# A sigmoid attention with a SwiGLU block: who issues the loads of v, one transfer for each load, and the order inside the first quad

## The chip, the cores and the metric

The kernel runs on one NeuronCore of a Trainium2 chip. The metric is the device time of one execution in microseconds; lower is better. In this document PE is TensorE (PEld its weight loads), DVE is VectorE, ACT is ScalarE, SP is SyncE. SP does no arithmetic here: it issues almost all DMAs, one after the other, in the order in which the program lists them.

## The reference

```python
scores = (q @ k.T) / sqrt(64) - log(448)          # for each of 4 batches and 12 heads, 448 positions
attn   = sigmoid(scores)                          # no softmax, so no sum over a row
x      = (attn @ v), heads side by side           # 1792 tokens x 768
xn     = x / sqrt(mean(x*x) + 1e-6) * rms_g
out    = (silu(xn @ w_gate) * (xn @ w_val)) @ w_out   # d_ff 1536
```

q, k and v come as float32, the weights as 64-bit words that the kernel turns into float32 itself.

## The kernel before, in words

**Units.** Four heads of one batch make a unit; there are 12, u = 0 to 11. Two heads lie side by side on the partitions (r = 0, 1 are the two pairs of heads of a unit). For each unit the kernel loads q and k (`load_qk`, lines 192 to 193) and v (`load_v`, lines 200 to 201). Both go through `load` (lines 186 to 190), which makes two DMAs, one for each r, of 224 KB each, both on SP. Unit 0 alone takes its q and k by `load_first` (lines 195 to 198), in pieces that hold both r at once, 128 to 256 KB.

**q and k on their way.** DVE splits them into two float16 parts (`qk_hi` L227, `qk_lo` L231). The parts are then transposed: for the first units on PE (`on_pe`, L263), from unit 3 on by one DMA transpose for each unit (`transpose_both`, L234), issued by SP too. I call these transposes T(3) to T(11). `scores` (L282) needs the transposed tile.

**Steps.** Each unit has 7 steps (c = 0 to 6). The main loop (lines 900 to 922) takes two steps at a time: first the scores of steps n and n+1 (24 small PE products), each followed on ACT by a sigmoid (L286), then the products with v of steps n-2 and n-1 (`av`, L297, 16 products). The scores have two PSUM buffers ("sc"), so the scores of step s wait for the sigmoid of step s-2. Between steps stand the parts of the list `FILL` (lines 853 to 861: the splits, transposes and loads of later units) and whatever `run_later` (lines 805 to 820) draws by its credits from the queues of additions, norms and weight splits.

**v.** There are two buffers for v, `v_b[u % 2]`. When the last product of unit u is listed, `av` calls `load_v(u + 2)` (lines 307 to 308). The load waits until that product has been done. On SP it is listed behind what was listed earlier: T(u+2) at step 3 of unit u, then k and q of unit u+4 at step 4, and only then v of unit u+2. Right behind the call the squares and scaled copies of the unit that just ended are run on ACT (`evict`, L316 and L319).

**Quads.** After the attention, 24 quads (one for each block of 128 columns of d_ff and each of two groups of batches) compute gate and value by seven products in place of eight (`quad`, lines 543 to 617; one product is nine PE instructions, L532). A quad takes its first product into the PSUM tile `pb` ("cb"), runs `fill(0)`, takes the second into the same tile, runs `fill(1)`, takes the third into `pd` ("cd"), runs `fill(2)`, takes the fourth into `pa` ("ca"), and so on. In the first quad, (0, 0), `fill` (lines 933 to 944) runs the norm of the last batch: `fill(0)` begins with its sums of squares on PE (`ssq`, L354), which need additions on DVE (L322) that follow the last products of the attention, and `fill(2)` holds the PE product that spreads the norm (`rinv`, L392).

**Start.** Lines 878 to 893 list the first loads on SP: q and k of unit 0 in pieces, v of unit 0, q and k of unit 1, the norm's weights, then units 2, 3 and the first weights.

Of the kernel before, what the change touches and what calls it, by code (L numbers as in the profile page):

```python
# [24 lines left out]
def attention_then_swiglu(  # L25
# [21 lines left out]
    nc = tc.nc  # L47
    B, H, S, D = q.shape
    DFF, DM = w_out.shape
    P = 128  # L50
# [53 lines left out]
    def words(of, at, *shape, dt=F32):  # L104
        n = math.prod(shape) if dt != F16 else math.prod(shape) // 2
        t = of[:, at : at + n]
        if dt != F32:
            t = t.bitcast(dt)
        names = " ".join("abcdef"[: len(shape)])
        sizes = dict(zip("abcdef", shape))  # L110
        return t.rearrange(f"p ({names}) -> p {names}", **sizes)
# [19 lines left out]
    v_b = [words(room, at0 + n * UW // 2, 2, NSLOT, D) for n in range(2)]  # L131
# [41 lines left out]
    def bank(name):  # L173
        return ps_m.tile([P, 512], F32, tag="m", name=name)

    def banks(name):
        return ps_s.tile([P, 2, 512], F32, tag="sc", name=name)
# [5 lines left out]
    at, pav = {}, {}  # L183
    PARTS = ((0, 0), (0, 1), (1, 0))

    def load(src, dst, u):
        b, n = divmod(u, NPAIR // 2)
        for r in range(2):
            rows = src[b, 4 * n + 2 * r : 4 * n + 2 * r + 2].rearrange("h s d -> (h s) d")
            nc.sync.dma_start(dst[:, r], rows.rearrange("(p c) d -> p c d", p=P))  # L190

    def load_qk(u, t):
        load((q, k)[t], (raw_b if u < 2 else ld_b)[u % 2][:, t], u)

    def load_first(t, *pieces):
        rows = (q, k)[t][0, :4].rearrange("(r h) s d -> r (h s) d", r=2).rearrange("r (p c) d -> p r c d", p=P)
        for begin, n in pieces:
            nc.sync.dma_start(raw(0, t)[:, :, begin : begin + n], rows[:, :, begin : begin + n])

    def load_v(u):  # L200
        load(v, v_b[u % 2], u)


    g_row = x_b[2][:NCC, 0, :P]
# [15 lines left out]
    def raw(u, t):  # L220
        return (raw_b if u < 2 else ld_b)[u % 2][:, t]
# [68 lines left out]
    def av(u, c):  # L290
        a = at.pop((u, c))
        if c == 0:
            pav[u] = [bank("av") for _ in range(2)]
        for r, ps in enumerate(pav[u]):
            for j in range(2):
                rows = slice(PB * j, PB * j + PB)
                nc.tensor.matmul(  # L297
                    ps[D * (j ^ r) : D * (j ^ r) + D, :S],
                    v_b[u % 2][rows, r, c],
                    a[rows, r],  # L300
                    start=(c == 0),
                    stop=(c == NSLOT - 1),
                )
        if c == NSLOT - 1:
            for r, ps in enumerate(pav.pop(u)):
                evict(u, r, ps)
            if u + 2 < NU:
                load_v(u + 2)
# [214 lines left out]
    def run_behind():  # L523
        if behind:
            behind.pop(0)()

    def product(ps, fc, n, a, b, more=False):

        w = win[fc % 2]
        for c in range(NK):  # L530
            for m, (l, r) in enumerate(PARTS):
                nc.tensor.matmul(  # L532
                    ps,
                    w[:, l, b, c],
                    xc[n, a][:, r, c],
                    start=(not more and c == 0 and m == 0),
                    stop=(c == NK - 1 and m == 2),
                    skip_group_check=more,
                )

    y_of = []

    def quad(fc, n, fill, whole=False):
        y = y_b[len(y_of) % 3]
        y_of.append((fc, n))
        pb = bank("cb")
        product(pb[:, :S], fc, n, 0, 0)
        nc.scalar.activation(y[:, 0], pb[:, :S], AF.Copy)  # L548
        run_behind()
        run_behind()  # L550
        fill(0)
        run_behind()

        product(pb[:, :S], fc, n, 4, 5, True)
        nc.scalar.activation(y[:, 1], pb[:, :S], AF.Copy)  # L555
        run_behind()
        fill(1)
        pd = banks("cd")[:, 0]
        product(pd[:, :S], fc, n, 5, 2)
        run_behind()  # L560
        fill(2)

        pa = bank("ca")

        def m2():
            product(pa[:, :S], fc, n, 1, 1)

        def gate():
            tt(g_b, pa[:, :S], y[:, 0], ALU.add)

        def silu():
            nc.scalar.activation(g_b, g_b, AF.Silu, scale=UNIT)

        def m7():
            product(pb[:, :S], fc, n, 3, 4, True)
            nc.scalar.activation(c_b, pb[:, :S], AF.Copy)  # L576

        def c22():
            tt(c_b, pd[:, :S], c_b, ALU.add)

        def m4():
            product(pb[:, :S], fc, n, 6, 3, True)
            stt(y[:, 0], pb[:, :S], SH * UNIT, g_b, ALU.mult, ALU.mult)

        def m3():
            product(pd[:, :S], fc, n, 2, 6, True)
            tt(y[:, 1], pd[:, :S], y[:, 1], ALU.add)  # L587

        def silu_1():
            nc.scalar.activation(y[:, 1], y[:, 1], AF.Silu, scale=UNIT)  # L590

        def ends():
            stt(y[:, 1], c_b, SH * UNIT, y[:, 1], ALU.mult, ALU.mult)
            i, m = fc % 2, fc // 2
            nc.sync.dma_start(
                y_d[n * NTOK : n * NTOK + NTOK, :, i, m].rearrange("t p x -> p t x"),
                y.rearrange("p j s -> p (j s)").rearrange("p (t x) -> p t x", x=P),
            )

        if whole:  # L600
            m7()
            c22()
            m2()
            gate()
            silu()
            fill(3)
            m4()
            m3()
            fill(4)
            behind.extend((wait, wait, wait, silu_1, ends))  # L610
        else:
            m2()
            fill(3)
            m7()
            gate()
            fill(4)
            behind.extend((silu, c22, m4, lambda: (m3(), silu_1()), ends))
# [215 lines left out]
    K, Q = 1, 0  # L833
# [36 lines left out]
    with tc.manual_schedule():  # L870
# [7 lines left out]
        warm(WARM)  # L878
        load_first(Q, *PIECES)
        load_first(K, *K_PIECES)  # L880
        load_v(0)
        load_qk(1, Q)
        load_qk(1, K)
        load_g()
        load_qk(2, K)
        load_qk(2, Q)
        load_v(1)
        load_w(0, 0)
        load_w(0, 1)
# [10 lines left out]
        for n in range(0, len(todo) + 2, 2):  # L900
# [14 lines left out]
            if n in SPLIT_AT:  # L915
                fc = SPLIT_AT.index(n)
                split[fc] = split_w(fc)
                first, second = split[fc]
                splits.extend(first[:4])
            if n in REST_AT:  # L920
                first, second = split[REST_AT.index(n)]
# [11 lines left out]
        def fill_norm(where):  # L933
            left = LEFT[where]

            def fill(at):
                run_load()
                while len(later) > left[at]:
                    later.pop(0)[0]()
                for part, *_ in third[: EARLIER[where][at]]:  # L940
                    part()
                del third[: EARLIER[where][at]]

            return fill
# [3 lines left out]
        def fill_steps(*steps):  # L948
            def fill(at):
                for p in steps[at]:  # L950
                    if p == fed[0]:
                        load_a(p, 0)
                        fed[0] += 1
                    else:
                        for part in split_a(p, 0):
                            part()

            return fill

        def fill_with(*steps):  # L960
            def fill(at):
                run_load()
                run_load()
                for part, *_ in steps[at]:
                    part()

            return fill
# [4 lines left out]
        for fc, n in order:  # L972
            if (fc, n) in LEFT:
                fill = fill_norm((fc, n))
            elif (fc, n) == (1, 1):
                assert len(third) == 8
                fill = fill_with(third[:2], third[2:4], third[4:7], third[7:], [])
            elif fc + 1 < NFC:
                first, second = split[fc + 1] = split_w(fc + 1) if n == 0 else split[fc + 1]
# [13 lines left out]
                fill = fill_with(*parts)  # L993
            elif n == 0:
                assert not outs
                fill = fill_steps([0, 1, 2], [], [0, 3, 1], [2], [4, 5])
            else:
                fill = fill_steps([3, 6], [], [4], [], [5, 6])
# [78 lines left out]
```

## Time and profile before

| | |
|---|---|
| time, median of 3 runs | 572.67 us (570.92 to 573.28) |
| the profiled execution's own time | 572.34 us |
| its span, first to last instruction | 570.5 us |
| outside the span | 1.84 us |
| PE busy | 561.1 us, 98% |
| DVE busy | 437.8 us, 77% |
| ACT busy | 265.6 us, 47% |
| PE clock granted | 1.00 throughout |
| attention | 5 to 135 us |
| quads | 135 to 423 us |
| output product | 423 to 570 us |

The attention is the stretch in which all engines and the DMAs work beside each other; in the quads and the output product PE runs without a break. A line of a timeline gives the start, the duration, the engine and line, and in brackets how long the engine had been idle before it and who ended that. For a DMA the duration on SP is the time of issuing, not of the transfer.

### The profile page before, as it was taken

Reading aid. Unit: us, or ns where it says so; the run is one execution under the profiler, and the core shown is the slowest. Engines: PE = TensorE matmul, PEld = TensorE weight load, DVE = VectorE, ACT = ScalarE, POOL = GpSimd, SP = SyncE. Lnnn points to the kernel's source line nnn. Section 1 sums busy time; section 2 is a strip of 40 time slices with the busy share of each in tenths; the row PEclk is TensorE's granted clock in tenths of the full one; section 3 lists DMA queues with packets and bytes.
Section 4 is the critical chain, followed back from the end, with each engine's and each line's share of the span. In section 5 each row is a group of like instructions: output and inputs, shape, how many; then the busy total and the mean of one; then the engine's idle time right before and its main releaser. Section 6 shows DMA issues by size and latency. Waiting matters only on the chain.

```text
span 570.5 us, 10232 instructions
## 1 busy us (share of the span) xinstructions
PE 561.1 (98%) x4224; PEld 305.2 (54%) x4224; DVE 437.8 (77%) x577; ACT 265.6 (47%) x398; POOL 0.7 (0%) x6
## 2 busy tenths in 40 slices
PE   8999989999999999999999999999999999999997
PEld 5555545554555555555555555555556666666664
DVE  4898889989886777878778787787567987777751
ACT  5788888885544243252442524425438342222220
POOL 0000000000000000000000000000000000000000
PEclk9999999999999999999999999999999999999999
DMA  7999999990017446364563745633426476444211
GB/s 247 258 260 230 224 258 236 197 207 1 19 48 198 139 148 172 103 186 131 154 169 102 192 126 157 168 99 94 143 73 220 141 227 200 150 151 143 59 41 43
DMA packets 99201, 87.25 MB, mean 153 GB/s; under 512 B 38735, under 2 KB 92242, under 8 KB 99154
## 3 DMA queue, kind: packets, MB, share of 16 engines
q1 hardware_dynamic: 98594, 85.91, 57.3%
q8 instruction: 33, 0.54, 0.4%
q10 hardware_dynamic: 560, 0.69, 0.3%
q14 instruction: 14, 0.11, 0.1%
HBM read 61.34 MB, written 16.52 MB: 136 GB/s over the span
## 4 chain that ended last, share of the span: by engine, by line
PE 90%; DVE 4%; DMA 3%; ACT 1%; SPq 1%; issue 1%; ACTq 0%; DVEq 0%
PE cb L532 28%; PE cd L532 14%; PE av L297 8%; PE oc L735 7%; PE o L735 7%; PE od L735 7%; PE ca L532 7%; PE sc L282 6%; PE ob L735 4%; DVE room L396 1%; DMA room<-in_v_dram 1%; DMA room<-in_q_dram 1%; DMA xc<-in_k_dram 1%; SPq L190 1%; ACT room L286 1%; PE ssq L354 1%
## 5 line engine op out<-in xcount | busy, mean ns | idle before, releaser
L532 PEld LDWEIGHTS <-wr 128*128 128x128 f16 x1512 | 147.8, 98 | 138.6 <-issue 1.0
L532 PE MATMUL cb<-xc,wr 128*128 128x448 f16 x756 | 147.3, 352 | 0.0
L286 ACT ACTIVATE room<-sc 128x896 f32<-128x896 f32 x84 | 75.2, 929 | 18.4 <-PE sc L282 17.7
L297 PE MATMUL av<-room 64*64 64x448 f32 x672 | 74.7, 538 | 1.4 <-DMA room<-in_v_dram 1.4
L532 PE MATMUL cd<-xc,wr 128*128 128x448 f16 x324 | 65.2, 352 | 0.0
L282 PE MATMUL sc<-xc 64*64 64x448 f16 x1008 | 59.9, 351 | 1.7 <-ACT room L286 1.0
L282 PEld LDWEIGHTS <-xc 64*64 64x64 f16 x1008 | 32.5, 106 | 30.9 <-issue 19.0
L587 DVE TENSOR_TENSOR room<-cd,room 128x448 f32<-128x448 f32 x24 | 15.0, 625 | 43.1 <-PE cd L532 43.1
L735 PEld LDWEIGHTS <-xc 128*128 128x128 f16 x360 | 35.2, 98 | 23.3
L502 DVE SCALAR_TENSOR_TENSOR wr<-wr 128x1536 f16<-128x1536 f32 (+3 forms) x28 | 37.3, 1355 | 12.5 <-ACT wr L499 12.5
L532 PE MATMUL ca<-xc,wr 128*128 128x448 f16 x216 | 44.8, 352 | 0.0
L735 PE MATMUL o<-room,wr 128*128 128x384 f16 x252 | 41.1, 326 | 0.0
L297 PEld LDWEIGHTS av<-room 64*64 64x64 f32 x672 | 27.8, 133 | 24.2 <-issue 16.9
L555 ACT ACTIVATE room<-cb 128x448 f32<-128x448 f32 x24 | 13.1, 544 | 53.8 <-PE cb L532 53.8
L576 ACT ACTIVATE room<-cb 128x448 f32<-128x448 f32 x24 | 13.1, 544 | 50.6 <-PE cb L532 30.6
L735 PEld LDWEIGHTS <-room 128*128 128x128 f16 x270 | 26.4, 98 | 17.5
L590 ACT ACTIVATE room<-room 128x448 f32<-128x448 f32 x24 | 13.8, 577 | 43.2 <-DVE room L587 43.2
L499 ACT ACTIVATE wr<-wr 128x768 f16<-128x768 f32 (+1 forms) x48 | 33.5, 754 | 0.0
L735 PEld LDWEIGHTS <-wr 128*128 128x128 f16 x252 | 24.7, 98 | 16.3
L690 ACT ACTIVATE xc<-xc 128x1536 f16<-128x1536 f32 (+1 forms) x12 | 14.5, 1260 | 36.2 <-DVE xc L687 36.2
L496 DVE TENSOR_TENSOR wr<-wr 128x384 f32<-128x384 f32 x48 | 26.4, 552 | 0.7
L548 ACT ACTIVATE room<-cb 128x448 f32<-128x448 f32 x24 | 13.1, 545 | 25.5 <-PE cb L532 25.5
(98 smaller groups left out, 676.0 us busy)
## 6 DMA issues: line engine op xcount, KB each, us to landing
y_d<-room SPq DMA_DIRECT2D x24, 448.0 KB, 3.3
xc<-in_moe_w_out_dram SPq DMA_DIRECT2D x12, 768.0 KB, 6.3
xc<-y_d SPq DMA_DIRECT2D x22, 384.0 KB, 4.4
room<-in_v_dram SPq DMA_DIRECT2D x24, 224.0 KB, 4.2
out_dram<-room SPq DMA_DIRECT2D x49, 96.0 KB, 2.2
wr<-in_moe_w_gate_dram SPq DMA_DIRECT2D x12, 384.0 KB, 4.5
wr<-in_moe_w_gate_dram SPq DMA_DIRECT2D x24, 192.0 KB, 5.0
wr<-in_moe_w_val_dram SPq DMA_DIRECT2D x12, 384.0 KB, 5.7
```

What stands on the lines that cost most here:

```text
L282: nc.tensor.matmul(o, T[rows, 1, l, c, cols], T[rows, 0, m, :, cols], start=(n == 0), stop=(n == 2))
L286: nc.scalar.activation(a, ps[:, :, :S], AF.Sigmoid, bias=-math.log(S), scale=1.0 / (math.sqrt(D) * SQ * SQ))
L297: nc.tensor.matmul(ps[D * (j ^ r) : D * (j ^ r) + D, :S], v_b[u % 2][rows, r, c], a[rows, r], start=(c == 0), stop=(c == NSLOT - 1),)
L496: first.append((lambda o=o, f0=f0, f1=f1: tt(wf[:, o], wf[:, f0], wf[:, f1], ALU.subtract), 0.6))
L499: nc.scalar.activation(t[:, 0, s], wf[:, s], AF.Copy, scale=SW)
L502: stt(t[:, 1, s], wf[:, s], SW, t[:, 0, s], ALU.mult, ALU.subtract)
L532: nc.tensor.matmul(ps, w[:, l, b, c], xc[n, a][:, r, c], start=(not more and c == 0 and m == 0), stop=(c == NK - 1 and m == 2), skip_group ...
L548: nc.scalar.activation(y[:, 0], pb[:, :S], AF.Copy)
L587: tt(y[:, 1], pd[:, :S], y[:, 1], ALU.add)
L590: nc.scalar.activation(y[:, 1], y[:, 1], AF.Silu, scale=UNIT)
L690: return lambda: nc.scalar.activation(s[:, 0, a:b], f[:, a:b], AF.Copy), 0.0, ()
L735: nc.tensor.matmul(ps[:, :HALF], a(m, l), w(m, r), start=(not more and m == 0 and n == 0), stop=(m == NM - 1 and n == 2), skip_group_check ...
```

## The change

Three things are changed. `load` makes one DMA for both r, and takes the queue as an argument; v of the units 4 to 8 is issued by ACT, at the place in the program where SP issued it. At the start q of unit 1 is listed ahead of v of unit 0. In the first quad the product into `pd` is taken second, with `fill(0)` run after its first three of nine instructions, and `fill(2)` moves behind the product into `pa`.

```diff
-    def load(src, dst, u):
+    def load(src, dst, u, queue=nc.sync):
         b, n = divmod(u, NPAIR // 2)
-        for r in range(2):
-            rows = src[b, 4 * n + 2 * r : 4 * n + 2 * r + 2].rearrange("h s d -> (h s) d")
-            nc.sync.dma_start(dst[:, r], rows.rearrange("(p c) d -> p c d", p=P))
+        rows = src[b, 4 * n : 4 * n + 4].rearrange("(r h) s d -> r (h s) d", r=2)
+        queue.dma_start(dst, rows.rearrange("r (p c) d -> p r c d", p=P))
...
     def load_v(u):
-        load(v, v_b[u % 2], u)
+        load(v, v_b[u % 2], u, nc.scalar if 3 < u < 9 else nc.sync)
...
-    def product(ps, fc, n, a, b, more=False):
+    def product(ps, fc, n, a, b, more=False, mid=None):
...
                     skip_group_check=more,
                 )
+            if c == 0 and mid:
+                mid()
...
         product(pb[:, :S], fc, n, 0, 0)
         nc.scalar.activation(y[:, 0], pb[:, :S], AF.Copy)
-        run_behind()
-        run_behind()
-        fill(0)
-        run_behind()
+        pd = banks("cd")[:, 0]
+        first = not y_of[1:]
+        if first:
+            product(pd[:, :S], fc, n, 5, 2, mid=lambda: fill(0))
+        else:
+            run_behind()
+            run_behind()
+            fill(0)
+            run_behind()
 
         product(pb[:, :S], fc, n, 4, 5, True)
         nc.scalar.activation(y[:, 1], pb[:, :S], AF.Copy)
         run_behind()
         fill(1)
-        pd = banks("cd")[:, 0]
-        product(pd[:, :S], fc, n, 5, 2)
-        run_behind()
-        fill(2)
+        if not first:
+            product(pd[:, :S], fc, n, 5, 2)
+            run_behind()
+            fill(2)
...
             m2()
+            if first:
+                fill(2)
             fill(3)
             m7()
             gate()
...
         load_first(K, *K_PIECES)
+        load_qk(1, Q)
         load_v(0)
-        load_qk(1, Q)
         load_qk(1, K)
```

## Rows read from the trace of the kernel before

**Rows 1.** Windows view, 56 to 86 us: stretch, length, busy time of each engine, clock, DMA.
```profile
56.00:86.00 30.00, 27.82 (x379) 15.49 (x371) 25.85 (x36) 25.98 (x40) 0.00 (x0) 1.00 1.11 244
```

**Rows 2.** Timeline of PE, 62 to 101 us: start, us, line, idle before and releaser.
```profile
62.79 1.30 PE L282 MATMUL sc<-xc 64*64 64x448 f16 x24
...
69.90 0.76 PE L282 MATMUL sc<-xc 64*64 64x448 f16 x12 [0.61 <-ACT room L286]
...
72.31 1.33 PE L282 MATMUL sc<-xc 64*64 64x448 f16 x24
...
77.71 2.03 PE L297 MATMUL av<-room 64*64 64x448 f32 x14 [1.43 <-DMA room<-in_v_dram]
...
97.39 1.30 PE L282 MATMUL sc<-xc 64*64 64x448 f16 x24
...
100.03 1.30 PE L282 MATMUL sc<-xc 64*64 64x448 f16 x24
```

**Rows 3.** Timeline of all engines at two places, 65 and 86 us.
```profile
65.12 0.14 PEld L297 LDWEIGHTS av<-room 64*64 64x64 f32 x2 [0.30 <-DMA room<-in_v_dram]
...
86.20 1.33 PE L282 MATMUL sc<-xc 64*64 64x448 f16 x24
```

**Rows 4.** Timeline of SP's queue, 48 to 80 us: duration is the time of issuing.
```profile
48.62 7.65 SPq L234 DMA_TRANSPOSE xc<-room  x1
...
59.25 0.85 SPq L190 DMA_DIRECT2D room<-in_v_dram  x2
...
62.42 7.88 SPq L234 DMA_TRANSPOSE xc<-room  x1
70.36 1.04 SPq L190 DMA_DIRECT2D xc<-in_k_dram  x2
...
72.45 0.85 SPq L190 DMA_DIRECT2D room<-in_v_dram  x2
73.39 6.14 SPq L234 DMA_TRANSPOSE xc<-room  x1
```

**Rows 5.** Source view of L234, the transpose issued at 62.42 alone.
```profile
DMA to landing us min/median/max: 9.8/9.8/9.8
```

**Rows 6.** Timeline of ACT, 54 to 82 us.
```profile
54.08 0.54 ACT L316 ACTIVATE room<-av 128x448 f32<-128x448 f32 x1 [1.31 <-PE av L297]
...
65.25 0.55 ACT L316 ACTIVATE room<-av 128x448 f32<-128x448 f32 x1
...
66.76 0.92 ACT L286 ACTIVATE room<-sc 128x896 f32<-128x896 f32 x1 [0.44 <-PE sc L282]
...
80.79 1.73 ACT L286 ACTIVATE room<-sc 128x896 f32<-128x896 f32 x2 [1.76 <-PE sc L282]
```

**Rows 7.** Source views of L198 and L797: issue durations ns, min/median/max.
```profile
L198 SPq DMA_DIRECT2D room<-in_q_dram x2: 450/455/460, 0.7 to 1.3; - x2
...
L797 ACTq DMA_DIRECT2D out_dram<-room x7: 496/497/557, 479.3 to 567.0; - x7
```

**Rows 8.** Timeline at 552 us: one DMA issue on SP and one on ACT.
```profile
552.42 0.47 SPq L797 DMA_DIRECT2D out_dram<-room  x1
552.42 0.50 ACTq L797 DMA_DIRECT2D out_dram<-room  x1
```

**Rows 9.** Timelines of PE and DVE, 135 to 141 us, the first quad.
```profile
135.00 1.88 PE L532 MATMUL cb<-xc,wr 128*128 128x448 f16 x9
137.24 0.95 PE L354 MATMUL ssq<-ones,room 128*112 128x1 f32 x8 [0.37 <-DVE room L322]
138.05 1.86 PE L532 MATMUL cb<-xc,wr 128*128 128x448 f16 x9
139.75 1.87 PE L532 MATMUL cd<-xc,wr 128*128 128x448 f16 x9
...
136.56 0.63 DVE L322 TENSOR_TENSOR room<-room,xc 128x448 f32<-128x448 f32 x1
```

**Rows 10.** Timeline of DVE at 10 us: the first split of q of unit 1.
```profile
9.97 0.63 DVE L227 TENSOR_SCALAR room<-room 128x896 f16<-128x896 f32 x1 [0.19 <-DMA room<-in_q_dram]
```

## The prediction

> **What bounds the kernel now.** I read the busy time by stretch first. From the quads on PE has no gap, so only the attention and the seam to the first quad can give anything. In the attention the stretch from 56 to 86 us is the poor one: PE is busy for 27.82 of 30 us, and ACT for 25.98 [rows 1], so ACT is close behind PE. The timeline of PE tells what a pair of steps costs when nothing is late: 100.03 - 97.39 = 2.64 us [rows 2]. Between 62.79 and 86.20 [rows 2, 3] PE does seven pairs, 7 x 2.64 = 18.48, and eight sums of squares (about 0.8, as 138.05 - 137.24 in [rows 9]), 19.3 in all; it takes 23.41. So 4.1 us are lost there. The brackets name the losers: PE waits 0.30 for v of unit 5 at 65.12, 0.61 for ACT at 69.90, and 1.43 for v of unit 6 at 77.71 [rows 2, 3].
>
> Then SP's queue, to see why v is late. The products of unit 4 were done by 65.25, when ACT squared them [rows 6]; from then on v of unit 6 could be loaded. It was issued at 72.45, because the transpose T(6) held SP from 62.42 to 70.30 and k and q of unit 8 came next [rows 4]. So 7.2 us of lateness are the queue's order, not the transfer's.
>
> Last, ACT. From its sigmoid at 66.76, late by 0.44 since v of unit 5 had upset the order of products on PE, it works without idling until 80.79 - 1.76 = 79.03, then idles 1.76 because PE stood waiting for v [rows 6]. What PE can gain here is therefore what ACT's chain of 79.03 - 66.76 = 12.27 us allows.
>
> **v of units 4 to 8 on ACT.** v of unit 6 is issued at about 65 in place of 72.45 and lands well before 76. Unit 5's is issued at 54 in place of 59.25. With v of unit 5 in time, PE takes the next scores 2.64 after 62.79, at 65.43, and the sigmoid that began at 66.76 has its 12 products some 0.75 later, at 66.2: 0.57 earlier. ACT's 12.27 us then end at 78.5, and with no wait for v the next sigmoid starts there, not at 80.79: 2.3 gained. PE also ran its products out of step from 78 to 84; with those in step I take 2.8 of the 4.1. Bounds: 1.8 (ACT loses only its idle time of 1.76), 4.1 (all).
>
> The price on ACT is five issues of 0.50 [rows 7]. For v of unit 6 ACT must wait until PE has done unit 4, then issues, and its square at 65.25 comes hardly later. At 54.08 ACT had idled 1.31 waiting for PE, so the issue falls behind that wait and delays the square by 0.5, of which about half reaches PE through the next sigmoid. Each of the five lies between 0 and 0.5; I take 0.15 on average, 0.75 together. v of unit 4 lands in time too, which gives back 0.35, about one group of four products (a quarter of 1.5). No row shows an issue on ACT beside a transpose on SP; the third rival prices that.
>
> **One transfer for each load.** The nearest row for the issue of a transfer of both r is `load_first`'s 0.455 [rows 7]; two halves cost 0.85 to 1.04 [rows 4]. SP gets back about 0.5 for each k and q, and all of v's 0.85 where ACT issues it. Before T(6) that is k and q of unit 7 and v of unit 5, 1.9, and as much again before T(5), for k and q of unit 6 and v of unit 4: T(6) is issued some 3 us earlier. T(6) landed at 62.42 + 9.8 = 72.2 and PE's scores at 72.31 had waited for it [rows 2, 4, 5]. v of unit 6 now crosses while T(6) is under way; its 448 KB at the 244 GB/s of this stretch [rows 1] are 1.9 us of the engines. 3 - 1.9 still leaves T(6) about 1 us ahead, which is what the 2.8 needs. If the transfers bind and T(6) stays at 72.2, only 1.8 remain. The bytes and the size of their pieces don't change, so the DMA engines get nothing back. A product with v now waits for both r, which costs nothing where v is early. From 86 on PE is dense and T(8) to T(11) move with SP.
>
> **q of unit 1 ahead of v of unit 0.** DVE waited 0.19 for that q [rows 10]; it is first on the queue now. 0.2 gained; bounds 0 and 0.2. v of unit 0 lands where q did, 9.94, over 2 us before its first product.
>
> **First quad.** PE idles before `ssq`, which waits for an addition that ends at 137.19. A product takes 139.75 - 138.05 = 1.70, so the first one ended at 136.70 and 0.54 were lost [rows 9] (the row's bracket says 0.37, since it lets the last product end later). Three of the nine instructions of the moved product, 0.57, fill the gap: `ssq` starts at 137.27. Nothing is added: the same nine are gone from their old place. `rinv` comes about as late as before (1.70 + 0.57 + 0.8 + 1.13 + 1.70 + 1.70 = 7.6 after 135.00, so 142.6 against 141.45); ACT and DVE use it only behind other work. 0.5 gained; bounds 0.3 and 0.55. If DVE should lag PE by more, the cover of 0.57 is too short and the rest of the lag is paid as before.
>
> **Sum.** 2.8 + 0.35 - 0.75 + 0.2 + 0.5 = 3.1. The profiled execution took 572.34 (span 570.5 and 1.84 around it), 0.33 below the median of the runs shown. 572.34 - 3.1 = **569.2**. A measurement of this kernel can tell about 0.5% from no change, 2.9 us; against the median that is below 569.8.
>
> **Rivals.**
> 1. *The transfers bind.* T(6) comes no earlier, since v of unit 6 shares the engines with it. For it: a DMA share above 1 in this stretch [rows 1]. Against it: SP issues without a break, so the queue's order alone explains the lateness. Then 1.8 replaces 2.8: 570.2, no change.
> 2. *ACT becomes the bound.* The issues are not hidden: 5 x 0.5 = 2.5 in place of 0.75, while ACT is busy 26 of 30 us [rows 1]. Then 572.34 - 1.35 = 571.0, no change.
> 3. *ACT's issue waits for SP's transpose.* Where SP is inside a transpose, ACT would stand until that has been issued: at 54.08 until 48.62 + 7.65 = 56.27, at 65.25 until 70.30, and for v of unit 7, about 10 us later at 75.3, until 73.39 + 6.14 = 79.53 [rows 4, 6]: 2.2 + 5.0 + 4.2 = 11.4 on an engine that is the next bound. ACT's idle times cover 1.31 + 0.44 + 1.76 = 3.5 of it, and the 0.7 of the last two parts stay: 572.34 + 7.9 - 0.7 = 579.5, slower. It decides as soon as the issue on ACT takes more than about 1 us. Against it: at 552.42 SP and ACT issue at the same time, 0.47 and 0.50, neither longer than alone [rows 7, 8]; but neither is a transpose, and with T moved ahead by 3 us the waits shrink. The Trainium skill, Perfetto Trace Analysis, section "DMA Instruction — HWDGE (DVE, Sync)", says that the block which makes the descriptors is shared by two sequencers and locked by one for its own use; by that rule this rival is the forecast and the time is its 579.5, but the two equal rows at 552.42 don't show it.
> 4. *The loads are as late as before.* If ACT reached its issue no earlier than SP did, nothing in the attention would move: 572.34 - 0.7 = 571.6. Nothing speaks for it, as ACT's square at 65.25 stands right behind the place of the issue.
>
> **Chances.** Forecast 0.52 (from 567.3, with all of the 4.1, the price on ACT down to 0.2 and 0.55 in the quad, to 569.8), rival 1 0.18, rival 2 0.14, rival 3 0.12, rival 4 0.04. The range of 8 in 10 takes in rivals 1, 2 and 4, which end at 571.6, and a share of the noise: 567.3 to 572.2. Faster by over 0.5%: 0.52; within 0.5%: 0.36; slower: 0.12.
>
> **What would show it.** Right: in the new trace the five issues on ACT take about 0.5 each, v of unit 6 is issued near 65 and PE has no wait for v; the pair of steps that began at 86.20 begins near 83.6 (86.20 less 2.8 + 0.35 - 0.75 + 0.2); SP's transpose T(6) begins near 59; `ssq` follows the three products without idling. Wrong: an issue on ACT of several us (rival 3); PE waiting for the transposed tile near 72 (rival 1); PE waiting longer for ACT at 48 to 60 and near 70 (rival 2).

## The result, and the profile after

| | kernel before | changed kernel |
|---|---|---|
| time, median of 12 runs each, on the same chip | 572.5 us (569.81 to 574.81) | 575.46 us (574.16 to 578.22) |
| ratio to before, 95% interval | | 1.0051 [1.0032, 1.0071] |
| the profiled execution: time, span | 572.34, 570.5 us | 575.54, 573.8 us |

The changed kernel is slower by 0.5%. The forecast was 569.2, with a range up to 572.2: wrong in sign and outside the range.

The windows view of the changed kernel, with the columns of [rows 1], shows in which stretch the time goes.

```profile
20.00:56.00 36.00, 34.49 (x506) 18.49 (x501) 29.92 (x58) 28.59 (x42) 0.00 (x0) 1.00 1.16 246
56.00:86.00 30.00, 25.24 (x338) 12.30 (x334) 22.93 (x33) 23.21 (x37) 0.00 (x0) 0.94 1.01 227
86.00:135.00 49.00, 49.00 (x712) 24.88 (x708) 45.93 (x77) 42.29 (x61) 0.00 (x0) 1.00 0.85 184
```

From 86 us on PE is dense, as before. In the stretch that was to gain, PE does 25.24 us of work in place of 27.82 [rows 1], ACT 23.21 in place of 25.98, and PE's clock averages 0.94 of full speed. Both engines do less: neither is the bound there, and something made them wait.

The timeline of PE in the changed kernel, from 51 us:

```profile
51.15 1.33 PE L281 MATMUL sc<-xc 64*64 64x448 f16 x24
...
54.04 0.98 PE L296 MATMUL av<-room 64*64 64x448 f32 x8
...
61.13 0.76 PE L281 MATMUL sc<-xc 64*64 64x448 f16 x12 [3.47 <-ACT room L285]
62.46 0.94 PE L281 MATMUL sc<-xc 64*64 64x448 f16 x12 [0.57 <-ACT room L285]
63.13 3.26 PE L296 MATMUL av<-room 64*64 64x448 f32 x16
66.32 0.55 PE L391 MATMUL rinv<-room,ones 112*128 112x448 f16 x2
66.80 1.33 PE L281 MATMUL sc<-xc 64*64 64x448 f16 x24
67.96 1.67 PE L296 MATMUL av<-room 64*64 64x448 f32 x16
69.47 1.30 PE L281 MATMUL sc<-xc 64*64 64x448 f16 x24
```

PE waits 3.47 and 0.57 us for ACT's sigmoids, and then 16 products with v take 3.26 us where 16 others take 1.67 three rows further on. The scores at 69.47 are those that began at 62.79 before [rows 2]: 6.68 us later. To see what ACT was doing, its timeline in the changed kernel, at two places:

```profile
44.02 1.85 ACTq L189 DMA_DIRECT2D room<-in_v_dram  x1
...
45.91 0.54 ACT L315 ACTIVATE room<-av 128x448 f32<-128x448 f32 x1 [1.04 <-issue]
...
52.84 0.91 ACT L285 ACTIVATE room<-sc 128x896 f32<-128x896 f32 x1
59.30 0.38 ACTq L189 DMA_DIRECT2D room<-in_v_dram  x1
59.73 0.54 ACT L315 ACTIVATE room<-av 128x448 f32<-128x448 f32 x1 [5.98 <-DMA xc<-in_k_dram]
60.17 0.91 ACT L285 ACTIVATE room<-sc 128x896 f32<-128x896 f32 x1
```

The bracket at 59.73 is the finding. ACT did nothing for 5.98 us, and what released it was neither PE nor the load of v that it was about to issue, but a load of **k**. The issue of v of unit 5 itself took 0.38 us; it stood ahead of the square of unit 3, which stood ahead of the sigmoids that PE needed. The source view of the load function, cut to the one load of k that SP issued at 54.60, says who waited for it:

```profile
L189 SPq DMA_DIRECT2D xc<-in_k_dram x1: 588/588/588, 54.6 to 54.6; - x1
...
  ACT room L315: 6.0, 1
...
DMA to landing us min/median/max: 4.6/4.6/4.6
```

54.60 + 4.6 = 59.2, and ACT issues at 59.30. That is k of unit 7, which has nothing to do with v of unit 5. The compiled program has the reason. Three rows of its listing, with the semaphores that each waits for (the first two rows are SP's, the last is ACT's; the number in front only counts the rows of the listing):

```
30 L189 DMA room<-in_v_dram 128x2x448 [waits DMAHW5_49,PE_49]
38 L189 DMA xc<-in_k_dram 128x2x448 [waits DMAHW6_49]
52 L189 DMA room<-in_v_dram 128x2x448 [waits DMAHW6_49,DMAHW5_49,PE_49]
```

The DMAs of SP and ACT are given eight completion semaphores in turn, DMAHW0 to DMAHW7, and the program lets each issue wait until the transfer that had its semaphore before has landed. On a single queue this only asks that the transfer eight places earlier has landed. In the order of the program, counted over both engines, v of unit 5 (row 52) is the eighth DMA behind k of unit 7 (row 38), so it takes the same DMAHW6. The other two waits are right ones: DMAHW5 is v of unit 3 (row 30), whose buffer it overwrites, and PE's last product with that buffer, done at 54.04 + 0.98 = 55.02.

What the 6.68 us consist of: 0.97 came earlier (from 20 to 56 us PE is busy for 34.49 us, against 35.45 before), since the issue of v of unit 4 took 1.85 us at 44.02, beside three issues of weights on SP (2.02 us from 44.02), and the scores that began at 50.18 in the kernel before began at 51.15. The two waits are 3.47 + 0.57 = 4.04. The rest is PE's clock. Below are that row of the kernel before and the windows view of the changed kernel:

```profile
50.18 1.33 PE L282 MATMUL sc<-xc 64*64 64x448 f16 x24
```

```profile
62.00:64.00 2.00, 1.54 (x20) 0.93 (x23) 1.12 (x2) 2.00 (x4) 0.00 (x0) 0.73 1.36 174
64.00:66.00 2.00, 2.00 (x16) 0.48 (x8) 0.04 (x1) 0.99 (x2) 0.00 (x0) 0.50 1.23 166
...
62.40:66.30 3.90, 3.84 (x28) 1.40 (x27) 1.16 (x2) 2.59 (x5) 0.00 (x0) 0.57 1.17 168
```

After the long wait the granted clock is 0.50, that is 1.2 GHz in place of 2.4, for some 3 us; over the 3.90 us from 62.40 it averages 0.57, which costs 3.90 x 0.43 = 1.7. Together 0.97 + 4.04 + 1.7 = 6.7.

From there on the stretch gains what was forecast. The other three issues on ACT:

```profile
71.60 0.37 ACTq L189 DMA_DIRECT2D room<-in_v_dram  x1
81.09 0.37 ACTq L189 DMA_DIRECT2D room<-in_v_dram  x1
92.18 0.38 ACTq L189 DMA_DIRECT2D room<-in_v_dram  x1
```

and the timeline of PE at the end of the stretch and in the first quad:

```profile
90.02 1.33 PE L281 MATMUL sc<-xc 64*64 64x448 f16 x24
...
139.06 1.88 PE L531 MATMUL cb<-xc,wr 128*128 128x448 f16 x9
140.78 0.73 PE L531 MATMUL cd<-xc,wr 128*128 128x448 f16 x3
141.34 0.91 PE L353 MATMUL ssq<-ones,room 128*112 128x1 f32 x8
142.12 1.30 PE L531 MATMUL cd<-xc,wr 128*128 128x448 f16 x6
```

The scores of 86.20 [rows 3] begin at 90.02, +3.82: of 6.68 us, 2.86 were won back. `ssq` follows its three products without idling. The first quad begins 4.06 later than in [rows 9], and the span ends 3.3 later.

### The profile page after: what moved, and what is told of

Its sections match the earlier page's. It is cut to its first block, busy times and chain, and to the rows that moved or that the text cites. A ratio compares the mean times of both kernels' runs of the same rounds, so it can differ in the third digit from the quotient of the medians.

```text
span 573.8 us, 10166 instructions
## 1 busy us (share of the span) xinstructions
PE 561.7 (98%) x4224; PEld 304.0 (53%) x4224; DVE 437.5 (76%) x577; ACT 265.7 (46%) x398; POOL 0.7 (0%) x6
## 4 chain that ended last, share of the span: by engine, by line
PE 92%; ACT 4%; issue 1%; DMA 1%; DVE 1%; SPq 0%; ACTq 0%
PE cb L531 29%; PE cd L531 14%; PE av L296 9%; PE oc L743 7%; PE od L743 7%; PE o L743 7%; PE ca L531 7%; PE sc L281 6%; PE ob L743 4%; ACT room L285 2%; DMA xc<-in_k_dram 1%; ACT room L318 1%; PE tr L262 1%; PE ssq L353 0%; PE warm L884 0%
## 5 line engine op out<-in xcount | busy, mean ns | idle before, releaser
L296 PE MATMUL av<-room 64*64 64x448 f32 x672 | 73.2, 548 | 0.0
L281 PE MATMUL sc<-xc 64*64 64x448 f16 x1008 | 58.5, 351 | 6.7 <-ACT room L285 6.1
L296 PEld LDWEIGHTS av<-room 64*64 64x64 f32 x672 | 26.2, 135 | 23.3 <-issue 19.0
```

The source lines that it names most:

```text
L281: nc.tensor.matmul(o, T[rows, 1, l, c, cols], T[rows, 0, m, :, cols], start=(n == 0), stop=(n == 2))
L296: nc.tensor.matmul(ps[D * (j ^ r) : D * (j ^ r) + D, :S], v_b[u % 2][rows, r, c], a[rows, r], start=(c == 0), stop=(c == NSLOT - 1),)
```

## The experiments

Three theories run through them. **A:** ACT works in order, and the issue of v of unit 5 stands until an unrelated load has landed. **B:** every issue on ACT costs something, or stands while SP is inside a transpose (the third rival). **C**, from the fifth run on: v of unit 5 on ACT is bad whatever it waits for, because it lands late (the text of the first run has another C). The first four stood beside runs of the kernel before with a median of 573.5 us, the next four beside 573.95, the last three beside 573.18.

**All of v back on SP** (the single transfers, the start and the quad stay).

```diff
-        load(v, v_b[u % 2], u, nc.scalar if 3 < u < 9 else nc.sync)
+        load(v, v_b[u % 2], u, nc.sync)
```

> The changed kernel with all of v issued by SP; one transfer for each load, the new start and the new first quad stay. Theory A (ACT stands because its issue of v of unit 5 waits for the landing of k of unit 7, whose completion semaphore it shares): no issue on ACT, so none of the 5.2 us wait and none of the 1.85 us issue; the quad (0.65) and the start (0.2) stay gained and v of unit 6 is still issued behind T(6), so 571.0, some 4.5 below the changed kernel. Theory B (an issue on ACT stands while SP makes the descriptors of a transpose): the same 571. Theory C (the merged loads are what costs: a product waits for both halves): 575, as slow as the changed kernel.

Measured: 568.79 us, ratio 0.9904 [0.9884, 0.9925]. So ACT's issues are what makes the change slow, and without them it is clearly faster than before, by more than the forecast for the whole change. It is also 2.2 below the 571.0 that A and B expected, since they took v of unit 6 to stay late behind T(6); the C of this text, that the single transfers cost, falls.

**Without v of units 4 and 5**, and **without unit 5 alone**.

```diff
-        load(v, v_b[u % 2], u, nc.scalar if 3 < u < 9 else nc.sync)
+        load(v, v_b[u % 2], u, nc.scalar if 5 < u < 9 else nc.sync)
```

> The changed kernel with only v of units 6 to 8 on ACT, 4 and 5 back on SP. Theory A: the wait of 5.2 us and the issue of 1.85 go, and the 2.8 us that early v of unit 6 gave in the changed kernel stay: 569.5, faster than both. Theory B: the transposes now come while ACT wants to issue, ACT stands 1 to 5 us for v of unit 6 and 7: 572 to 576.

```diff
-        load(v, v_b[u % 2], u, nc.scalar if 3 < u < 9 else nc.sync)
+        load(v, v_b[u % 2], u, nc.scalar if u in (4, 6, 7, 8) else nc.sync)
```

> The changed kernel with v of unit 5 alone back on SP. Theory A: all of the 5.2 us wait goes, the 1.2 us that v of unit 4 cost stay: 570.7. Theory B: little changes against the changed kernel, since units 4, 6, 7, 8 still issue on ACT: 573 to 576.

Measured: 569.67 us (ratio 0.994 [0.9905, 0.9975]) and 569.8 us (0.9922 [0.9902, 0.9941]). Putting back one load of five gives 5.7 us between the two medians (6.7 when each is held against the kernel before that ran beside it). With units 6 to 8 on ACT the issues take 0.44, 0.41 and 0.38 us, though v of unit 6 is issued at 64.43 inside a transpose that SP issues from 58.32 to 64.96: B falls as far as it makes ACT stand for the transpose. Unit 4's issue takes 1.27 us here, and PE is busy for 34.99 of the 36 us from 20 in place of 35.46 without it; the two medians don't show these 0.5 us. Nothing is gained over SP either.

**v of units 4 to 8 on GpSimd**, which computes nothing in this stretch.

```diff
-        load(v, v_b[u % 2], u, nc.scalar if 3 < u < 9 else nc.sync)
+        load(v, v_b[u % 2], u, nc.gpsimd if 3 < u < 9 else nc.sync)
```

> The changed kernel with v of units 4 to 8 issued by GpSimd, which has nothing else to do in the attention, in place of ACT. Theory A: whatever the issue waits for, nobody stands behind it, and GpSimd's DMAs have completion semaphores of their own: v is early, ACT loses nothing, 569.0, the fastest. Theory B: the same, unless GpSimd's issue is slow. Against both: if v through GpSimd lands over 9 us after its issue, PE waits for v and the time is 572 or more.

Measured: 569.25 us, 0.9938 [0.9912, 0.9964], but with executions from 568.55 to 574.75. The profiled one is the slowest of ten; there the transposes at 47.32 and 60.41 took 9.07 and 10.24 us to issue, against 7.65 and 7.88 in [rows 4], and PE waited 3.46 us for a transposed tile. GpSimd's timeline in that execution, at v of unit 5:

```profile
54.13 0.72 POOL L189 DMA_DIRECT2D room<-in_v_dram  x1 [9.08 <-PE av L296]
```

PE's last product with that buffer ended there at 52.78 + 0.98 = 53.76, and GpSimd, whose DMAs have semaphores of their own in the compiled program, issues 0.4 later, before SP issues k of unit 7 at 56.44: PE alone held it. So this load does not have to wait for k, an idle engine takes ACT's wait away, and it too gains nothing over SP.

**v of unit 5 alone on ACT.**

```diff
-        load(v, v_b[u % 2], u, nc.scalar if 3 < u < 9 else nc.sync)
+        load(v, v_b[u % 2], u, nc.scalar if u == 5 else nc.sync)
```

> The changed kernel with v of unit 5 alone on ACT, the other eleven on SP. Theory A (ACT takes its work in order, and its issue of v of unit 5 stands until k of unit 7 has landed on SP's queue, since the two loads are given the same one of eight completion semaphores): nearly all of the loss comes back with this one load. ACT idles some 5 us, issues near 59 us, PE waits over 3 us for ACT; the time is that of the changed kernel less what v of unit 4 cost (about 1), some 574.3 us, between 573.3 and 575.3. Theory B (every load on ACT costs something alike, and the loss is their sum): one of five, some 570 us.

Measured: 575.91 us (574.62 to 578.17), 1.0039 [1.0017, 1.0061]. One load costs as much as the five did. That is 1.6 more than I expected, and 0.6 above the range. The trace (of an execution of 577.13) shows a part of the reason: k of unit 7 is issued at 56.19 in place of 54.60, since v of unit 4 is on SP again (0.55) and T(5) takes 8.69 to issue in place of 7.87, and the wait lasts longer. ACT's timeline and, below it, the source view of that load of k:

```profile
61.00 0.43 ACTq L189 DMA_DIRECT2D room<-in_v_dram  x1
61.48 0.54 ACT L315 ACTIVATE room<-av 128x448 f32<-128x448 f32 x1 [8.41 <-DMA xc<-in_k_dram]
```

```profile
  ACT room L315: 8.4, 1
...
DMA to landing us min/median/max: 4.7/4.7/4.7
```

56.19 + 4.7 = 60.9, and ACT issues at 61.00: it moves with the landing of k, again 0.1 behind it.

**Another load in front on the semaphore.** The three loads of the second block's w_val go to GpSimd, so the round over the eight semaphores has three DMAs fewer between; and the control, the same with v on SP.

```diff
-        loads.extend((fc, lambda d=d, x=x: nc.sync.dma_start(d, x)) for d, x in zip(sides(dst), src))
+        loads.extend((fc, lambda d=d, x=x: (nc.gpsimd if (fc, kind) == (1, 1) else nc.sync).dma_start(d, x)) for d, x in zip(sides(dst), src))
```

> The changed kernel, all five loads of v on ACT as there, but the three loads of w_val of the second block are issued by GpSimd in place of SP. With three loads fewer in the round, the load that had the semaphore of v of unit 5 before it is no longer k of unit 7 but the last of three loads of w_gate, which landed at 53.7 us. Theory A (the shared completion semaphore is the cause): v of unit 5 is issued at 54 to 55 us, ACT does not idle 6 us there, and the time stands within 1.5 us of the same kernel with v on SP, which runs beside it. Theory C (v of unit 5 on ACT is bad whatever it waits for, since it then crosses a transpose and lands 11 us after its issue): PE waits 3 to 5 us for v near 60 us, and the time stands 3 us or more above that kernel.

> The kernel with all of v on SP in single transfers, and the three loads of w_val of the second block on GpSimd: the control for the run beside it. SP gets back 2.3 us before the transpose T(6). Both theories: between 567.5 and 569.5 us, since in the kernel with w_val on SP no wait of PE for v or a transposed tile was left in this stretch.

In the compiled program v of unit 5 now takes DMAHW3, behind the last of three loads of w_gate (the first row is SP's, the second ACT's):

```
36 L463 DMA wr<-in_moe_w_gate_dram 64x3x256 [waits DMAHW3_49]
52 L189 DMA room<-in_v_dram 128x2x448 [waits DMAHW5_49,DMAHW3_49,PE_49]
```

Measured: 572.6 us (571.56 to 577.03) with v on ACT, ratio 0.9985 [0.9957, 1.0014]; 571.18 (570.22 to 572.03), 0.9944 [0.9914, 0.9975], for the control. They are 1.4 us apart, against 6.7 for the medians of the changed kernel and the one with all of v on SP. Below are ACT's timeline of the first one, where the wait was, and SP's issue of k of unit 7 with its landing:

```profile
45.01 3.47 ACTq L189 DMA_DIRECT2D room<-in_v_dram  x1
...
59.14 0.41 ACTq L189 DMA_DIRECT2D room<-in_v_dram  x1
59.60 0.54 ACT L315 ACTIVATE room<-av 128x448 f32<-128x448 f32 x1 [1.79 <-PE av L296]
```

```profile
57.82 0.58 SPq L189 DMA_DIRECT2D xc<-in_k_dram  x1
...
DMA to landing us min/median/max: 4.1/4.1/4.1
```

The long wait is gone; the square of unit 3 waits for PE, as it did at 54.08 in [rows 6]. k of unit 7 lands only at 57.82 + 4.1 = 61.9, and ACT issues v of unit 5 at 59.14, 2.8 us before that: without the shared semaphore the issue does not wait for k. The profiled execution is the second slowest of the ten (576.14 us), and it shows a part of C: v of unit 5 lands 12.8 us after its issue and PE waits 2.25 us for it at 71.97; and the issue of v of unit 4 takes 3.47 us. Both misses cost something in that execution; the median leaves 1.4 us for all of them. The control missed its expectation by 1.7 us; in its trace PE waits 0.48 and 1.38 us for v on SP, which it did not with w_val there.

**The single transfers alone**, on the kernel before.

```diff
-        for r in range(2):
-            rows = src[b, 4 * n + 2 * r : 4 * n + 2 * r + 2].rearrange("h s d -> (h s) d")
-            nc.sync.dma_start(dst[:, r], rows.rearrange("(p c) d -> p c d", p=P))
+        rows = src[b, 4 * n : 4 * n + 4].rearrange("(r h) s d -> r (h s) d", r=2)
+        nc.sync.dma_start(dst, rows.rearrange("r (p c) d -> p r c d", p=P))
```

> The kernel before with one transfer for each load and nothing else; all loads on SP. Theory A': the single transfers alone give most of the gain that the kernel with all of v on SP has over the kernel before (4.7 us), that is all but the 0.85 of the start and the first quad: some 569.6 us, between 568.8 and 570.4; T(6) is issued 2.5 to 3 us earlier and PE has no wait for v of unit 6. Rival: the single transfers do nothing by themselves (the bytes are the same), and the gain of the kernel with all of v on SP came from the start, whose order shifts the whole attention: 571.5 us or more.

Measured: 570.1 us (569.86 to 570.4), 0.9918 [0.9885, 0.995], 3.85 below the median of before: as expected. SP's queue, to be held against [rows 4], and PE's windows:

```profile
57.03 0.41 SPq L189 DMA_DIRECT2D room<-in_v_dram  x1
57.48 2.51 SPq L463 DMA_DIRECT2D wr<-in_moe_w_val_dram  x3
60.09 6.72 SPq L233 DMA_TRANSPOSE xc<-room  x1
66.86 0.58 SPq L189 DMA_DIRECT2D xc<-in_k_dram  x1
67.48 0.47 SPq L189 DMA_DIRECT2D xc<-in_q_dram  x1
68.05 1.31 SPq L189 DMA_DIRECT2D room<-in_v_dram  x1
```

```profile
56.00:86.00 30.00, 29.30 (x428) 15.49 (x420) 28.59 (x43) 28.31 (x43) 0.00 (x0) 1.00 1.14 271
```

T(6) is issued 2.3 us earlier, and v of unit 6 at 68.05 in place of 72.45. PE is busy for 29.30 of 30 us and waits for no load. The stretch that took 23.41 us in the prediction's count takes 20.53 here (the scores at 63.44 to those at 83.97), 2.88 less. What ACT was to cure, shorter issues on SP cure alone.

**The loads of v on ACT alone**, in halves, for units 6 to 8.

```diff
-    def load(src, dst, u):
+    def load(src, dst, u, queue=nc.sync):
...
-            nc.sync.dma_start(dst[:, r], rows.rearrange("(p c) d -> p c d", p=P))
+            queue.dma_start(dst[:, r], rows.rearrange("(p c) d -> p c d", p=P))
...
-        load(v, v_b[u % 2], u)
+        load(v, v_b[u % 2], u, nc.scalar if 5 < u < 9 else nc.sync)
```

> The kernel before, its loads in halves, its start and its first quad as they were; only v of the units 6, 7 and 8 is issued by ACT. This is the part of the change on which the prediction set most (v of unit 6 in time: 1.8 at the least, 2.8 of its 4.1). Theory D (the queue's order was the cause, and either cure, shorter issues on SP or another queue, brings the gain by itself): v of unit 6 is issued near 65 and PE does not wait for it, 569.5 to 570.5 us. Theory E (v of unit 6 then crosses T(6), which is still issued at 62.4; T(6) lands later than 72.2 and PE waits for it in place of v): 572 us or more, no gain without the single transfers.

Measured: 577.02 us (576.03 to 577.97), 1.007 [1.0043, 1.0097]. Both expectations missed the mechanism. D is wrong outright; E has the sign, but T(6) is not what PE waits for. It is A again, now with v of unit 6. Below are PE's timeline, ACT's timeline, and the source view of the three w_val loads that SP issued from 61.22 on, then of the second of them alone:

```profile
71.62 0.76 PE L282 MATMUL sc<-xc 64*64 64x448 f16 x12 [2.31 <-ACT room L286]
73.79 1.33 PE L282 MATMUL sc<-xc 64*64 64x448 f16 x12 [1.41 <-ACT room L286]
```

```profile
68.13 1.52 ACTq L190 DMA_DIRECT2D room<-in_v_dram  x2
69.69 0.54 ACT L316 ACTIVATE room<-av 128x448 f32<-128x448 f32 x1 [3.26 <-issue]
```

```profile
  ACT room L316: 3.3, 1
...
DMA to landing us min/median/max: 5.7/6.0/6.3
...
L464 SPq DMA_DIRECT2D wr<-in_moe_w_val_dram x1: 632/632/632, 61.7 to 61.7; - x1
...
DMA to landing us min/median/max: 6.3/6.3/6.3
```

61.70 + 6.3 = 68.0, and ACT issues at 68.13. With the loads in halves each takes two turns of the round, and in the compiled program the first half of v of unit 6 takes the semaphore of this second piece of w_val. The clock falls after PE's waits here too: 0.57 from 72 to 74 us and 0.50 from 74 to 78.

**Start and first quad alone**, and **all of v on SP once more**. The first is the changed kernel with `load` and `load_v` as they were before.

> The kernel before with only q of unit 1 ahead of v of unit 0 and the new order in the first quad; loads in halves, all on SP. The prediction has 0.2 + 0.5 for the two; the traces of the changed kernel show 0.18 and 0.65. So some 0.8 us below the kernel before. Rival: a shift of 0.2 at the start meets the same late transfers further on, and only the quad's part is left, 0.5 to 0.65.

> The changed kernel with all of v on SP once more, now in more rounds and beside the two other parts: single transfers (some 3.9) and start with first quad (0.8) add up, 4.7 us below the kernel before at the same time, between 4 and 6.7 below.

Measured: 571.7 us (570.62 to 578.86), 0.9984 [0.9957, 1.0011]: not told apart from no change, nor from the 0.8 expected. In its profiled execution (573.2) the first quad begins at 136.65, 1.65 later than in [rows 9], so a gain at the start did not last to there. 569.15 us (568.52 to 569.61), 0.9932 [0.9911, 0.9953]: 4.0 below before, at the lower end of what was expected. This kernel has the lowest medians of the study: faster than before by 0.7 to 1.0% in two comparisons, and faster than the changed kernel. The one with GpSimd is not told apart from it.

## Why the prediction was wrong

- **The step that failed**: "The price on ACT is five issues of 0.50 [rows 7] ... Each of the five lies between 0 and 0.5; I take 0.15 on average, 0.75 together." It priced how long an issue takes, and took it that ACT "must wait until PE has done unit 4, then issues". The issue has a further wait, for the last holder of its completion semaphore, and everything behind it on ACT waits along. Measured: 1.85, 0.38, 0.37, 0.37 and 0.38 us of issuing, and 4.3 us of ACT's waiting ahead of the second beyond what it waits for PE (PE's last product with that buffer runs from 54.04 to 55.02 in the changed kernel, the issue comes at 59.30; the text had "Unit 5's is issued at 54"). Through PE's waits (4.04) and its clock (1.7) that became some 5.7 us, where the prediction had 0.15 on average for one issue.
- **Rival 3** had the sign and the place, not the mechanism. At 59.30 SP was 1.1 us inside a transpose of 7.85, and the issue took 0.38; at 64.43 in the kernel with units 6 to 8 on ACT, 0.44. The rule of the Trainium skill, Perfetto Trace Analysis, section "DMA Instruction — HWDGE (DVE, Sync)", that one sequencer locks the block which makes the descriptors, cost nothing beside a transpose here, so these rows do not bear it out. Whether it, or something else, makes v of unit 4 slow to issue beside SP's weights (1.85, 1.27, 3.47 us in three kernels) was not tried; in the kernel with single transfers alone, SP itself has issues of 1.31 and 1.43 us with no other engine issuing.
- **Rivals 1, 2 and 4**: the transfers are not what cost the changed kernel its time, since PE waits for none there and the single transfers alone bring 3.85. They can bind in a single execution: PE waited 3.46 us for a transposed tile in the profiled one with GpSimd, and 2.25 us for v of unit 5 in the one with w_val on GpSimd. ACT is not the bound, it idles. Rival 4 came true for unit 5 alone: issued at 59.30 by ACT, at 59.25 by SP before.
- **+2.8 for the poor stretch**: right in size, 2.86 in the changed kernel, but by luck, since what brings it is another thing: the text gave it to v on ACT with T(6) "some 3 us earlier" as help. The runs show that the single transfers bring all of it alone (2.88), and that v of units 6 to 8 on ACT without them costs 3.8 (577.02 - 573.18). The two parts do not add; the one makes the other needless. T(6) too came out "about 1 us ahead" by two errors: it was issued 4.25 earlier (58.17) and took 13.2 to land in place of 9.8, so it landed at 71.4 against 72.2. And the 0.30 at 65.12 [rows 3] is the weight load's wait, not one of PE itself; of the 4.1 lost there, PE's own waits with a bracket are 0.61 and 1.43.
- **+0.35 for v of unit 4**: not seen; its issue cost PE 0.97 at that place.
- **+0.2 at the start**: the pair of 21.48 begins at 21.30, 0.18, and is not to be seen in the time. One trace cannot show it either: in the other kernels with the same order at the start that pair begins between 21.20 and 22.32.
- **+0.5 in the first quad**: the delay of the changed kernel falls from 4.06 at its first product to 3.3 at the end, 0.76, as `ssq` no longer idles. Right in sign and about in size, by the trace alone; the run of it by itself could not tell.

## What to carry to other kernels

Before a DMA moves to another engine's queue, list every semaphore that its issue will wait for, also those that the framework reuses, and price the wait as if all the work behind it on that engine stood still; an issue on an engine that computes is cheap only if all of these are done when the engine reaches it. Shortening the issues on the queue that is late (one transfer for both halves) can bring the same gain with no new wait. Parts of a change that cure the same lateness are not summed: try each alone.

## What the runs showed of the hardware that I had not expected

A load of the same 448 KB lands after very different times: k of unit 7, issued by SP at 54.60, in 4.6 us; v of unit 5, issued by ACT at 59.30 with T(6) just begun, in 11.1 us, and T(6) itself in 13.2 against 9.8 in [rows 5]. That the two cross is not enough to explain it: in the kernel with v of unit 5 alone on ACT they cross as well (T(6) issued at 60.17, v at 61.00) and land in 10.0 and 7.5 us. The cause stays open. The 3.47 us for which PE waited were followed by some 3 us at half the clock, so this wait on ACT cost PE about 1.7 us more than its length.
